# A third PSUM bank for the gated MLP's first-layer products, and the output weights' maximum ahead of the first group

## The chip, the cores and the metric

One core of one Trainium2 chip runs the whole kernel in one launch. The metric is the device time of that core in microseconds (us). Fewer is better. Three executions of the kernel before gave 2071.28, 2072.87 and 2073.14 us.

## The reference, cut to what matters

Three stages follow each other. The input of the first is 4 batches of 8 heads, 576 rows of 64 each. The second and third work on 2304 tokens of 512 features.

```python
# 1. attention with a threshold under each row's maximum
scores = q @ k.T / sqrt(64)
scores = where(scores >= max(scores) - tau, scores, -1e9)
x = softmax(scores) @ v                      # (2304, 512)
# 2. gated MLP
xn = x / rms(x) * rms_g
g, val = xn @ w_gate, xn @ w_val             # 512 -> 1536
x = (silu(g) * val) @ w_out                  # 1536 -> 512
# 3. eight experts, with weights P from a gate that is normalized eight times
out = sum(P[:, e] * (relu(x @ w1[e]) @ w2[e]) for e in range(8))
```

The change touches stage 2 and the place where it runs beside stage 1.

## The kernel before, in words

**Number format.** Every matrix is split into a high and a low fp16 part, and a product is three matmul passes (high by high, high by low, low by high; `passes`, line 546). The parts are scaled by powers of two. Each scale needs the largest value of a tensor over all partitions. `over_partitions` (line 127) gets it with one small matmul into PSUM and one VectorE maximum over it; from the second use on that matmul's tile has the tag `mx` in pool `psx`, with one buffer. This tile takes one bank of PSUM. All the kernel's small maxima share it: those of the keys and the values of each batch (`kmx`, `vmx`), of the output weights (`womx`), of the third stage's gate (`gmx`), and of its expert weights.

**Attention** runs tile by tile: 144 tiles, each of 128 query rows of one head (or of half as many rows of two heads). For a tile TensorE computes the scores `S` (line 303), VectorE their maximum (line 317), ScalarE the exponent `e` (line 321), VectorE the threshold and the sum (line 323), ScalarE the fp16 high part `hl` (line 328), POOL the low part (lines 329 and 330), a transposing DMA issued by SP turns it (`eT`, line 340), and four tiles later TensorE multiplies it by the values (`pv`, line 360). After 8 heads the row of 128 tokens is normalized and turned by another DMA into `xnT` (line 387).

**The gated MLP** works on groups of 256 tokens, nine in all. `mlp_in` (line 550) computes, for each of 12 blocks of 128 columns, `gv`: 12 matmuls for the gate and 12 for the value (line 557) into one PSUM bank of tag `mm` (pool `psm`, two buffers). ScalarE takes the tanh of the first half (line 565), and two VectorE operations form the gated product `u` (lines 566 and 567); the second of them is the last reader of the bank. ScalarE and POOL then split `u` into `tT` (lines 571 and 572). `mlp_out` (line 579) multiplies by the output weights into two tiles of the same tag `mm` (line 591). The first seven groups are given to the planner among the attention tiles; the last two come after attention and carry a `hook` that prepares expert weights.

**The weights' preparation** comes first. `prep_group` prepares the gate and value weights. `prep_out` (line 509) loads the output weights in 12 pieces (line 451, issued by SP), rebuilds them as 32-bit floats (lines 462 to 465), squares them on ScalarE for the row sums (line 517), forms the maximum `womx` (lines 519 to 527), and then scales and splits the 12 pieces (lines 534 to 536, VectorE, ScalarE and POOL).

**What sets the order.** The program is written down once, and a planner lays it out when the kernel is built: it takes for every engine the ready instruction with the lowest number, and numbers grow in the order of writing. It gives a PSUM buffer to a tile when one is free in its own estimate of the times. `high_priority(offset=n)` gives what stands in it numbers that are lower by `n`. Attention tiles get numbers as if no MLP work stood between them (`attention_order`), so that they go ahead of MLP work that is ready too. On the chip each engine then keeps this order and waits on semaphores. PSUM has eight banks: two tiles of two banks for `S`, one for `pv`, one for `mx`, two for `mm`.

Of the kernel before, what the change touches and what calls it, by code (L numbers as in the profile page):

```python
# [7 lines left out]
F32 = mybir.dt.float32  # L8
# [11 lines left out]
def kernel(  # L20
# [28 lines left out]
    E, _, FF = moe2_w1.shape  # L49
    P = 128  # L50
    KD = DM // P
    KF = DFF // P
# [8 lines left out]
    def small(shape, name, dt=F32, bufs=1):  # L61
        return p0.tile(shape, dt, tag=name, name=name, bufs=bufs)
# [63 lines left out]
    psx = ctx.enter_context(tc.tile_pool(name="psx", bufs=1, space=PSUM, side="left"))  # L126
# [12 lines left out]
    def all_max(col, name, first=False):  # L139

        return over_partitions(col.bitcast(BF16)[:, 1:2], ident, name, first)
# [26 lines left out]
    def norm_scale(sq, n, bits, name):  # L168

        return pow2_scale(sq, n, bits, name, 2.0**-60, True)  # L170
# [270 lines left out]
    NG = DFF // DM  # L441

    def words(src, name, tag="tT"):

        if tag == "tT":
            r = pw.tile([P, 4, 2, 2 * P], F16, tag=tag, name=name, bufs=4)
            r = r.rearrange("p f l n -> p (f l n)").bitcast(I32)
        else:
            r = pw.tile([P, 4, HD], F32, tag=tag, name=name)
            r = r.rearrange("p o d -> p (o d)").bitcast(I32)  # L450
        nc.sync.dma_start(out=r, in_=src)
        return r.rearrange("p (n w) -> p n w", w=2)

    def to_f32(dst, word, name):

        lw = pw.tile([P, 2, 2, HD], F16, tag="xs", name=name, bufs=2)  # L460
        lw = lw.rearrange("p o l n -> p (o l n)").bitcast(I32)
        A.activation(dst, word[:, :, 1].bitcast(F32), AF.Prelu, scale=2.0**-112, alpha=2.0**32)
        V.tensor_scalar(lw, word[:, :, 0], 29, None, ALU.logical_shift_right)
        di = dst.bitcast(I32)
        V.scalar_tensor_tensor(di, di, 3, lw, ALU.logical_shift_left, ALU.bitwise_or)
        return lw
# [42 lines left out]
    def prep_out():  # L509

        bits = moe_w_out.bitcast(I32)
        n = KF // NG
        om = small([P, KF], "om")
        for f in range(KF):
            wd = words(bits[f * P : (f + 1) * P, :], f"wo{f}", ("x2", "x2t")[f % 2])
            sq = to_f32(wo32[:, f], wd, f"wol{f}").bitcast(BF16)[:, 0:DM]
            A.activation(sq, wo32[:, f], AF.Square, accum_out=om[:, f : f + 1])
        for _ in range(2):
            V.tensor_tensor(
                om.rearrange("p (g f) -> p g f", g=NG),  # L520
                om.rearrange("p (g f) -> p g f", g=NG),
                igv.to_broadcast([P, NG, n]),
                ALU.mult,
            )
        om1 = small([P, 1], "om1")
        V.tensor_reduce(om1, om, AX.X, ALU.max)
        s, inv = norm_scale(all_max(om1, "womx"), 1, 9, "wout")
        V.tensor_scalar(ixs, inv, 2.0**10, None, ALU.mult)
        sf = small([P, NG], "wosf")
        V.tensor_scalar(sf, igv, s[:, 0:1], None, ALU.mult)  # L530
        rr = pw.tile([P, 4, HD], F32, tag="x2", name="wof")
        for f in range(KF):
            r = rr[:, f % 2 * 2 : f % 2 * 2 + 2].rearrange("p o d -> p (o d)")
            V.tensor_scalar(r, wo32[:, f], sf[:, f // n : f // n + 1], None, ALU.mult)
            A.activation(wo[:, f, 0, :], r, AF.Copy)
            G.tensor_tensor(wo[:, f, 1, :], r, wo[:, f, 0, :], ALU.subtract)

    NB = 2 * P
# [7 lines left out]
    def passes(n):  # L546

        return [(l, r, c) for c in range(n) for l, r in ((0, 0), (0, 1), (1, 0))]

    def mlp_in(j, hook=None):  # L550
        xt = xnT.pop(j)
        tT = []
        for f in range(KF):
            gv = psm.tile([P, 2, NB], F32, tag="mm", name=f"gv{j}_{f}")
            for a, w in enumerate((wg, wv)):
                for n, (l, r, kk) in enumerate(passes(KD)):
                    T.matmul(  # L557
                        gv[:, a, :],
                        lhsT=w[:, l, kk, f * P : (f + 1) * P],
                        rhs=xt[:, r * KD + kk, :],  # L560
                        start=n == 0,
                        stop=n == 3 * KD - 1,
                    )
            u = pw.tile([P, NB], F32, tag="u", name=f"u{j}_{f}", bufs=2)
            A.activation(u, gv[:, 0, :], AF.Tanh, scale=g32[f // (KF // NG)][:, 0:1])
            V.scalar_tensor_tensor(u, u, 1.0, gv[:, 0, :], ALU.add, ALU.mult)
            last = V.scalar_tensor_tensor(u, u, 2.0**-21, gv[:, 1, :], ALU.mult, ALU.mult)  # L567
            if f % 4 == 0:
                tq = pw.tile([P, 4, 2, NB], F16, tag="tT", name=f"tT{j}_{f}", bufs=4)
            t = tq[:, f % 4]  # L570
            A.activation(t[:, 0, :], u, AF.Copy)  # L571
            low = G.tensor_tensor(t[:, 1, :], u, t[:, 0, :], ALU.subtract)  # L572
            tT.append(t)
            if hook is not None:
                with tc.issue_after(last.ins), tc.issue_after(low.ins):
                    hook()
        return tT
# [65 lines left out]
    def attention_order():  # L643

        return tc.high_priority(offset=tc.cur_priority - first)
# [13 lines left out]
    def prepare(b, o):  # L659

        st = states[b]
        if o < NCH * H and o % H == 1:
            prep_q(st, o // H + 1)
        if b > 0 and o in (LAG - 3, LAG - 1):
            prep_v(st, (o - LAG + 3) // 2)
        if b + 1 == B:
            return
        nx = states[b + 1]
        early = b > 0
        if o == (4 if early else 20):  # L670
            nx["raw_k"] = load_raw("k", k, b + 1)
            nx["raw_v"] = load_raw("v", v, b + 1)
        for nm, o0, scales in (("k", 8 if early else 21, prep_k_scale), ("v", 11 if early else 24, prep_v_scale)):
            if o0 <= o < o0 + 3:
                row_norms(nx, nm, o - o0)
            if o == o0 + 2:
                scales(nx)
        o0 = 18 if early else 27
        if o0 <= o < o0 + 3:
            prep_k(nx, 0, o - o0)  # L680
        if o == 25:
            nx["raw_q"] = load_raw("q", q, b + 1)
        if o in (28, 29, 30):
            q_norms(nx, 2 * (o - 28), min(2 * (o - 27), NW))
        if o == 30:
            prep_q_scales(nx)
        if o == 32:
            prep_q(nx, 0)
        if o == 34:
            prep_k(nx, 1, 0)  # L690
        if o == 35:
            prep_k(nx, 1, 1)
            prep_k(nx, 1, 2)
# [20 lines left out]
    for t in range(len(row) + LAG):  # L714
        before = tc.cur_priority
        with attention_order():
            if t < len(row):
                b, c, heads, n, g = row[t]
                if n == 0:
                    g["sums"] = pa.tile([P, H], F32, tag="sums", name=f"sums{g['n']}", bufs=2)  # L720
                att_tile(states[b], c, heads, n, g)
                prepare(b, t % SLOTS)
            else:
                att_values(*waiting.pop(0))
                turn()
            done = list(ended)
            ended.clear()
            for g in done:
                (end_main if g["c"] < NCH else end_rem)(g)
        first += tc.cur_priority - before  # L730
        for g in done:
            i = g["i"]
            if i == 1:
                pse_cm.__exit__(None, None, None)
                psm = ctx.enter_context(
                    tc.tile_pool(name="psm", bufs=2, space=PSUM, side="right")
                )
                for gi in range(NG):
                    prep_group(gi)
                first = tc.cur_priority  # L740
                tT = mlp_in(0)
                prep_out()
                mlp_out(0, tT)
            elif i is not None and i % 2 == 1 and i < len(tiles) - 3:
                mlp_out(i // 2, mlp_in(i // 2))
# [211 lines left out]
    def hook():  # L957

        for call, *args in todo.pop(place[0], ()):
            call(*args)  # L960
        place[0] += 1

    j = NTL // 2 - 2
# [6 lines left out]
    tT = mlp_in(j + 1, hook)  # L970
# [206 lines left out]
    for hn in range(1, NE):  # L1177
        for which, base in ((1, 42 * (hn - 1) + 14 * (hn == 1)), (2, 42 * (hn - 1) + 21 + 13 * (hn == 1))):
            n = weight(which, hn, (lambda p: lambda: p)(w_pool(hn)))
# [5 lines left out]
    with tc.manual_schedule(engines={mybir.EngineType.PE}):  # L1185
        for k, (c, j) in enumerate(ahead):
            u, f = c // 2, c % 2
# [32 lines left out]
            while done < min(want, len(later)):  # L1220
                u, jj, j, _ = n = later[done]
# [51 lines left out]
```

## Time and profile before

| what | value |
|---|---|
| median of 3 executions | 2072.87 us (2071.28 to 2073.14) |
| the profiled execution's own time | 2072.64 us |
| its span, first to last instruction | 2070.8 us |
| TensorE (PE) busy | 1937.3 us, 94% |
| VectorE (DVE) busy | 1622.1 us, 78% |
| ScalarE (ACT) busy | 1297.6 us, 63% |
| POOL busy | 1351.4 us, 65% |

Attention fills the span from the start to about 597 us; the MLP's first matmul starts at 143.5 us and its last one at 728.2 us; the experts take the rest. A busy share is a mean over stages that have different limits, so the table says little by itself: what matters is, for the stretch in which the change acts, which engine stood idle and what released it. An operation is written as line, engine, operation, output <- inputs; what stands in square brackets behind an entry of the timeline is the idle time of the engine just before it and what ended it.

### The profile page before, as it was taken

Reading aid. Unit: us, or ns where it says so; the run is one execution under the profiler, and the core shown is the slowest. Engines: PE = TensorE matmul, PEld = TensorE weight load, DVE = VectorE, ACT = ScalarE, POOL = GpSimd, SP = SyncE. Lnnn points to the kernel's source line nnn. Section 1 sums busy time; section 2 is a strip of 40 time slices with the busy share of each in tenths; the row PEclk is TensorE's granted clock in tenths of the full one; section 3 lists DMA queues with packets and bytes.
Section 4 is the critical chain, followed back from the end, with each engine's and each line's share of the span. In section 5 each row is a group of like instructions: output and inputs, shape, how many; then the busy total and the mean of one; then the engine's idle time right before and its main releaser. Section 6 shows DMA issues by size and latency. Waiting matters only on the chain.

```text
span 2070.8 us, 43792 instructions
## 1 busy us (share of the span) xinstructions
PE 1937.3 (94%) x16462; PEld 1445.0 (70%) x16462; DVE 1622.1 (78%) x3364; ACT 1297.6 (63%) x2804; POOL 1351.4 (65%) x1412
## 2 busy tenths in 40 slices
PE   1558899899999998999999999999999999999998
PEld 0246676777777766777777777777777777777777
DVE  6998777778754546998888888888887888888865
ACT  6998778878753365657555555555555555555542
POOL 0457664666654476777677777776777777777754
PEclk9569999999999999999999999999999999999999
DMA  9987878977748665334434433444443434334332
GB/s 296 261 177 128 163 160 147 184 129 139 129 83 213 144 158 169 110 118 143 128 120 134 131 116 119 130 131 127 128 139 122 122 117 143 120 120 128 105 97 82
DMA packets 373093, 290.46 MB, mean 140 GB/s; under 512 B 286160, under 2 KB 299344, under 8 KB 372880
## 3 DMA queue, kind: packets, MB, share of 16 engines
q1 hardware_dynamic: 371712, 285.81, 53.6%
q8 instruction: 129, 2.11, 0.4%
q0 software_dynamic: 640, 1.84, 0.3%
q14 instruction: 84, 0.69, 0.1%
q10 hardware_dynamic: 528, 0.02, 0.0%
HBM read 195.71 MB, written 21.23 MB: 105 GB/s over the span
## 4 chain that ended last, share of the span: by engine, by line
PE 65%; DVE 3%; POOL 1%; DMA 1%; issue 1%; ACT 1%; SPq 0%; DVEq 0%; POOLq 0%; ACTq 0%
PE P L1127 30%; PE X L1059 17%; PE Z L1059 13%; PE gv L557 3%; PE x L591 2%; DVE w L766 1%; DMA xo<-x2d 1%; DVE acc L1141 0%; SPq L871 0%; DVE h L1038 0%; PE logits L913 0%; DVE lg L1005 0%; POOL w2s L833 0%; DVE w1m L790 0%; POOL h L1038 0%
## 5 line engine op out<-in xcount | busy, mean ns | idle before, releaser
L1127 PE MATMUL P<-w,h 128*128 128x256 f16 x6048 | 769.9, 273 | 2.7 <-DVE acc L1141 1.8
L1127 PEld LDWEIGHTS <-h 128*128 128x128 f16 x6048 | 591.4, 98 | 145.7 <-issue 9.8
L1059 PEld LDWEIGHTS <-w 128*128 128x128 f16 x4032 | 394.6, 98 | 195.6 <-issue 4.6
L1137 DVE SCALAR_TENSOR_TENSOR acc<-P,coef,acc 128x256 f32<-128x256 f32 x882 | 409.7, 477 | 81.7 <-PE P L1127 73.0
L1059 PE MATMUL X<-xo,w 128*128 128x384 f16 x2304 | 437.7, 327 | 1.3 <-ACT u2b L1079 0.9
L1059 PE MATMUL Z<-xo,w 128*128 128x384 f16 x1728 | 327.7, 326 | 1.5 <-DMA xo<-x2d 1.5
L329 POOL TENSOR_TENSOR hl<-e,hl 128x512 f16<-128x512 f32 x144 | 172.9, 1201 | 193.7 <-ACT hl L328 135.6
L557 PE MATMUL gv<-xnT,wg 128*128 128x256 f16 x1296 | 162.9, 274 | 14.7 <-DVE u L567 13.4
L557 PE MATMUL gv<-xnT,wv 128*128 128x256 f16 x1296 | 165.0, 273 | 0.0
L557 PEld LDWEIGHTS <-wg 128*128 128x128 f16 x1296 | 124.7, 98 | 33.7 <-issue 16.0
L591 PE MATMUL x<-wo,tT 128*128 128x512 f16 x648 | 144.2, 379 | 0.0
L323 DVE SCALAR_TENSOR_TENSOR e<-S,nt,e 128x576 f32<-128x576 f32 x144 | 116.5, 811 | 28.5 <-ACT e L321 28.0
L557 PEld LDWEIGHTS <-wv 128*128 128x128 f16 x1296 | 125.5, 98 | 14.7
L317 DVE TENSOR_REDUCE nt<-S 128x1 f32<-128x576 f32 x144 | 106.7, 750 | 25.1 <-PE S L303 22.8
L360 PE MATMUL pv<-vs,eT 128*128 128x64 f16 (+1 forms) x2240 | 97.1, 200 | 30.9 <-DMA eT<-hl 30.8
L360 PEld LDWEIGHTS <-eT 128*128 128x128 f16 (+1 forms) x2240 | 87.3, 105 | 52.9 <-DMA eT<-hl 40.3
L572 POOL TENSOR_TENSOR tT<-u,tT 128x256 f16<-128x256 f32 x108 | 74.9, 695 | 69.7 <-ACT tT L571 69.6
L321 ACT ACTIVATE e<-S,nt,c 128x576 f32<-128x576 f32 x144 | 117.4, 818 | 0.0
L591 PEld LDWEIGHTS <-tT 128*128 128x128 f16 x648 | 62.1, 98 | 70.7
L328 ACT ACTIVATE hl<-e 128x576 f16<-128x576 f32 x144 | 96.8, 677 | 21.3 <-DMA eT<-hl 10.4
L303 PE MATMUL S<-kT,qT 128*128 128x288 f16 (+1 forms) x320 | 65.2, 310 | 26.3 <-DVE e L323 19.7
L766 DVE SCALAR_TENSOR_TENSOR w<-w1r,w_s,w 128x512 f16<-128x512 f32 x64 | 84.1, 1328 | 7.1 <-ACT w L765 7.0
(2536 smaller groups left out, 3623.2 us busy)
## 6 DMA issues: line engine op xcount, KB each, us to landing
xo<-x2s SPq DMA_DIRECT2D x319, 384.0 KB, 3.1
w1r<-in_moe_w_dram SPq DMA_DIRECT2D x17, 1024.0 KB, 5.0
w2r<-in_moe_w_dram SPq DMA_DIRECT2D x17, 1024.0 KB, 6.1
x2s<-xo SPq DMA_DIRECT2D x17, 384.0 KB, 2.8
wgatew<-in_moe_w_gate_dram SPq DMA_DIRECT2D x12, 512.0 KB, 5.6
wo<-in_moe_w_out_dram SPq DMA_DIRECT2D x12, 512.0 KB, 4.6
wvalw<-in_moe_w_val_dram SPq DMA_DIRECT2D x12, 512.0 KB, 5.1
qX<-qT SPq DMA_DIRECT2D x40, 128.0 KB, 2.7
```

What stands on the lines that cost most here:

```text
L317: V.tensor_reduce(mx, sv, AX.XY, ALU.max)
L321: A.activation(ev, sv, AF.Exp, bias=nt[:, 0:1], scale=st["c2"][:, c : c + 1])
L323: V.scalar_tensor_tensor(ev, sv, nt[:, 1:2], ev, ALU.is_ge, ALU.mult, accum_out=sums[:, slot : slot + 1])
L328: A.activation(hl[:, 0:S], e, AF.Copy)
L329: G.tensor_tensor(hl[:, S + REM :], e[:, 0 : NCH * P], hl[:, 0 : NCH * P], ALU.subtract)
L360: T.matmul(o, lhsT=a, rhs=r, start=n == 0, stop=n == len(mm) - 1)
L557: T.matmul(gv[:, a, :], lhsT=w[:, l, kk, f * P : (f + 1) * P], rhs=xt[:, r * KD + kk, :], start=n == 0, stop=n == 3 * KD - 1,)
L591: T.matmul(ps, lhsT=tT[f][:, l, o : o + P], rhs=wo[:, f, r, :], start=n == 0, stop=n == 3 * KF - 1,)
L766: V.scalar_tensor_tensor(dst[1], src, s, dst[0], ALU.mult, ALU.subtract)
L1059: T.matmul(ps, lhsT=w[:, a, l, kk, f * P : (f + 1) * P], rhs=xb[:, r * 2 + kk, :], start=n == 0 and j in (0, 1, 3), stop=n == 5, skip_grou ...
L1127: T.matmul(ps, lhsT=hs[u, ao, f][:, l, jj * P : (jj + 1) * P], rhs=w2[h][:, bo, r, f, :], start=n == 0 and j in (0, 1, 3), stop=n == 5, sk ...
L1137: main[True] = V.scalar_tensor_tensor(y, ps, coef[h][:, i : i + 1], y, ALU.mult, ALU.add)
```

## The change

`mlp_in` without a hook, that is in the first seven groups, takes every third block's `gv` tile (f = 2, 5, 8 and 11) from pool `psx` with the tag `mx` instead of from `psm`. `prep_out` is cut in two: the first part ends with the maximum and returns the scale, the second (`split_out`) scales and splits. The first part is written ahead of the first group's `mlp_in`, whose instructions get the same numbers that the first part starts with; the second part stays behind it.

```diff
@@ prep_out
         s, inv = norm_scale(all_max(om1, "womx"), 1, 9, "wout")
         V.tensor_scalar(ixs, inv, 2.0**10, None, ALU.mult)
+        return s
+
+    def split_out(s):
+
+        n = KF // NG
         sf = small([P, NG], "wosf")
         V.tensor_scalar(sf, igv, s[:, 0:1], None, ALU.mult)
         rr = pw.tile([P, 4, HD], F32, tag="x2", name="wof")
@@ mlp_in
         for f in range(KF):
-            gv = psm.tile([P, 2, NB], F32, tag="mm", name=f"gv{j}_{f}")
+            if hook is None and f % 3 == 2:
+                gv = psx.tile([P, 2, NB], F32, tag="mx", name=f"gv{j}_{f}", bufs=1)
+            else:
+                gv = psm.tile([P, 2, NB], F32, tag="mm", name=f"gv{j}_{f}")
@@ the main loop
                 first = tc.cur_priority
-                tT = mlp_in(0)
-                prep_out()
+                p0_ = tc.cur_priority
+                so = prep_out()
+                with tc.high_priority(offset=tc.cur_priority - p0_):
+                    tT = mlp_in(0)
+                split_out(so)
                 mlp_out(0, tT)
```

## Rows read from the trace of the kernel before

**Rows 1.** Windows by stage: stretch, its length, busy us, clock, DMA share.

```profile
143.00:182.00 39.00, 32.46 (x377) 28.33 (x375) 34.12 (x87) 37.59 (x92) 33.58 (x38) 1.00 0.57 108
240.00:620.00 380.00, 362.62 (x4028) 278.59 (x4027) 283.94 (x660) 290.01 (x676) 234.40 (x324) 1.00 0.76 139
620.00:740.00 120.00, 119.15 (x909) 84.30 (x908) 59.25 (x132) 47.23 (x99) 55.63 (x69) 1.00 0.67 162
860.00:2071.00 1211.00, 1203.31 (x9259) 904.35 (x9256) 999.02 (x1945) 681.91 (x1418) 864.40 (x806) 1.00 0.40 122
```

**Rows 2.** Waits of TensorE, 140 to 620 us: total, times, longest.

```profile
PE gv L557 <- DVE u L567: 12.7, 13, 2.6
PE pv L360 <- DMA eT<-hl: 12.1, 15, 1.6
PE S L303 <- DVE e L323: 2.4, 4, 1.3
```

**Rows 3.** The tile gv: last reader of the bank.

```profile
L567 DVE SCALAR_TENSOR_TENSOR u<-u,gv x108: 404/420/422, 151.8 to 714.1; 128x256 f32<-128x256 f32 x108
```

**Rows 4.** Waits of TensorE, 140 to 240 us, then 240 to 620 us.

```profile
PE gv L557 <- DVE u L567: 6.1, 6, 2.6
...
PE gv L557 <- DVE u L567: 6.6, 7, 1.5
```

**Rows 5.** Timeline of TensorE, first group: start, length, instruction.

```profile
143.54 1.48 PE L557 MATMUL gv<-xnT,wg 128*128 128x256 f16 x12
...
146.16 0.27 PE L557 MATMUL gv<-xnT,wg 128*128 128x256 f16 x1
...
157.64 1.47 PE L557 MATMUL gv<-xnT,wg 128*128 128x256 f16 x12 [2.58 <-DVE u L567]
```

**Rows 6.** Timelines of SP and TensorE where the second group starts.

```profile
216.17 1.33 SPq L387 DMA_TRANSPOSE xnT<-xn  x1
...
219.40 1.49 PE L557 MATMUL gv<-xnT,wg 128*128 128x256 f16 x12 [1.08 <-DMA xnT<-xn]
```

**Rows 7.** Timeline of TensorE, two later waits and what follows each.

```profile
240.81 1.47 PE L557 MATMUL gv<-xnT,wg 128*128 128x256 f16 x12 [0.80 <-DVE u L567]
...
245.57 0.58 PE L360 MATMUL pv<-vs,eT 128*128 128x64 f16 x14 [1.36 <-DMA eT<-hl]
...
383.05 1.47 PE L557 MATMUL gv<-xnT,wg 128*128 128x256 f16 x12 [1.22 <-DVE u L567]
...
392.23 0.58 PE L360 MATMUL pv<-vs,eT 128*128 128x64 f16 x14 [1.60 <-DMA eT<-hl]
```

**Rows 8.** Timeline of TensorE where its clock falls once.

```profile
525.47 2.63 PE L557 MATMUL gv<-xnT,wg 128*128 128x256 f16 x12 [1.40 <-DVE u L567]
...
529.75 0.41 PE L303 MATMUL S<-kT,qT 128*128 128x288 f16 x2
```

**Rows 9.** Windows around it, columns as in rows 1.

```profile
522.00:526.00 4.00, 1.60 (x23) 1.08 (x21) 3.96 (x6) 1.33 (x4) 1.42 (x3) 0.95 0.40 83
526.00:530.00 4.00, 4.00 (x25) 3.00 (x24) 3.59 (x9) 2.52 (x7) 2.33 (x4) 0.62 1.05 177
```

**Rows 10.** Output weights: loads, rebuilding, squares, the maximum's matmul, the first piece's split.

```profile
L451 SPq DMA_DIRECT2D wo<-in_moe_w_out_dram x12: 328/460/575, 15.1 to 129.2; - x12
...
L465 DVE SCALAR_TENSOR_TENSOR wo<-wo,wol x12: 676/686/1636, 93.5 to 134.8; 128x512 int32<-128x512 int32 x12
L517 ACT ACTIVATE wol<-wo x12: 612/626/637, 95.0 to 136.5; 128x512 bf16<-128x512 f32 x12
...
L134 PE MATMUL womxp<-ident,om x1: 230/230/230, 138.3 to 138.3; 128*128 128x128 bf16 x1
...
L534 DVE TENSOR_SCALAR wof<-wo,wosf x12: 430/526/1367, 140.8 to 169.0; 128x512 f32<-128x512 f32 x12
```

**Rows 11.** Small maxima from 150 to 640 us: their matmuls, the keys' VectorE maximum.

```profile
L134 PE MATMUL vmxp<-ident,vmm x3: 219/219/220, 154.8 to 401.5; 128*128 128x128 bf16 x3
...
L134 PE MATMUL kmxp<-ident,kmm x2: 219/224/230, 215.9 to 355.7; 128*128 128x128 bf16 x2
L134 PE MATMUL gmxp<-ident,gm x1: 219/219/219, 436.5 to 436.5; 128*128 128x128 bf16 x1
...
L136 DVE TENSOR_REDUCE kmx<-kmxp x2: 285/289/293, 220.8 to 356.0; 128x1 f32<-128x128 f32 x2
```

## The prediction, made before the changed kernel was run

> **What bounds the kernel now.** I read the windows by stage first. From 860 us to the end TensorE is busy 1203.31 of 1211 us, and from 620 to 740 us, where the last MLP groups run alone, 119.15 of 120 us [rows 1]. There only less TensorE work, or work done earlier, can shorten the span. The stretch in which the change acts is the one before: from 240 to 620 us TensorE is busy 362.62 of 380 us, from 143 to 182 us 32.46 of 39 us [rows 1]. In that stretch MLP matmuls fill what attention leaves, and what is not done by 597 us is done after it, back to back. So a microsecond of TensorE idle time that goes before 620 us comes off the end, provided attention and the MLP's inputs keep up.
>
> Next the waits of TensorE between 140 and 620 us. Three kinds make up nearly all: a gv tile waits for the bank that VectorE's second product reads last, 12.7 us in 13 waits; values wait for a turned tile (eT), 12.1 us in 15; scores wait for the release of S, 2.4 us in 4 [rows 2]. Only the first kind is what a third bank addresses. It is 0.6% of the span, and the whole direct prize.
>
> **The third bank.** One gv block takes TensorE 146.16 - 143.54 = 2.62 us [rows 5]. With two banks, block f+2 may start once block f's second product has ended; that product lasts 0.42 us [rows 3], so a wait means that VectorE or ScalarE reached the block late in their queues. With three banks the release has one block more, at least 2.62 us. The longest wait is 2.58 us [rows 5], so in the old order of instructions every one of the 13 would vanish. What that brings at the end I count by place [rows 4].
>
> First place, 143 to 182 us: 6.1 us in 6 waits. ScalarE is busy 37.59 of 39 us there, TensorE 32.46 [rows 1]: ScalarE still serves the output weights' split beside attention and tanh. A further bank does not raise a rate that ScalarE sets; it lets TensorE get ahead by at most one block, 2.62 us. And that lead has to survive until the second group starts: its first matmul waits 1.08 us for an input that SP issues at 216.17 us [rows 6], so a first group that ends sooner meets the same late input unless attention comes sooner too. The bounds are 0 and -6.1 us; I take -1.0, near zero, because of the row at 219.40.
>
> The Trainium skill, "Perfetto Trace Analysis", section "Identifying the Most-Contended Engine", takes ScalarE's occupancy as a fair measure of its limit and says to work on the fullest engine first. By that the first place would be worth nothing, and the sum below would be 1.0 us smaller; by the waits alone it would be 5.1 us larger.
>
> Second place, 240 to 620 us: 6.6 us in 7 waits. Here no other engine is full (ScalarE 290.01, VectorE 283.94 of 380 us) [rows 1]. A wait is worth its length only if nothing late follows. After two of the seven, at 240.81 (0.80 us) and 383.05 (1.22 us), a value matmul waits for eT within 10 us, for 1.36 and 1.60 us [rows 7]. Its scores were made four attention tiles earlier, ahead of the gv wait, so eT will not come sooner, and these waits grow by what was gained. The other five are worth 6.6 - 0.80 - 1.22 = 4.58 us. The bounds are 0 (all five meet a late eT further on) and -6.6; I take -4.6.
>
> **The clock.** At 525.47 us a gv block after a wait of 1.40 us takes until 529.75, 4.28 us in place of 2.62 [rows 8, 5]. The granted clock of 526 to 530 us is 0.62, a mix of the levels 1.2 and 2.4 GHz; in the 4 us before TensorE was busy 1.60 us only [rows 9]. Without the 1.40 us of waiting TensorE is fuller ahead of that point and the clock may stay up. Bounds 0 and -1.7 us; I take half, -0.8.
>
> **New sharing.** From now on 28 gv tiles (four of each of seven groups) use the bank of the small maxima. In their time six maxima follow after 150 us: three of the values, two of the keys, one of the gate [rows 11]. None of their matmuls waits for a bank now. One can hold its bank long: a key maximum's matmul at 215.9 us is read only at 220.8, since VectorE had other work first [rows 11]. The price of one collision is bounded by 0 (the planner puts the small matmul where the bank is free, on the chip too) and by the longest wait for a gv bank, 2.58 us [rows 5]. I take one collision in all at the mean wait, 12.7 / 13 = 0.98 us [rows 2], so +1.0. Behind a waiting small matmul stand all TensorE work and, on VectorE, what follows the maximum: attention's next reductions. The scales themselves are not urgent: the batch that needs them begins many tiles later.
>
> **The moved maximum.** What moves ahead in number are 12 loads on SP, 24 ScalarE and 24 VectorE operations on them with their 12 sum readings, the few VectorE operations of the maximum and its matmul. On the chip they stand ahead of the first gv already: the last load is issued at 129.2 us, the last square starts at 136.5, the maximum's matmul at 138.3, the first split at 140.8 [rows 10], and gv starts at 143.54 [rows 5]. No DMA or POOL work of the first group is passed, since `mlp_in` issues none of the former and its POOL work stands behind the gv; POOL's work of the split stays behind in number. Against attention tiles from the twenty-first on the moved part gains rank, which can matter for its last load or two (0.46 us of SP each) [rows 10]. I cost the move at nothing; its cover is the late input of the first group. If that cover were gone, the third gv block could start only after the maximum.
>
> **The sum.** -1.0 - 4.6 - 0.8 + 1.0 = -5.4 us. Against the profiled execution's own 2072.64 us (span 2070.8, and 1.84 us around it; 0.23 us under the median) this gives **2067.2 us**, 0.26% less. Since the planner lays out the whole stretch anew, the 14.5 us of eT and score waits [rows 2] are dealt again; I leave their sum as it is.
>
> **Rivals.**
>
> *Attention keeps the pace (no change).* If ScalarE in the first place and eT later set the pace, each gv wait that goes comes back as an eT or input wait. For it: such a next wait stands in place already [rows 6, 7]. Against: ScalarE and VectorE have a quarter of their time free from 240 us on [rows 1], and after 525.47 nothing late follows for long. All bank terms are 0; 2072.6 us.
>
> *The shared bank (slower).* The small matmul of a maximum is queued on TensorE behind a gv block in the same bank, whose release hangs on VectorE. At the longest gv wait six maxima cost 6 x 2.58 = 15.5 us; with the other terms (-6.4) the time is 2072.64 + 9.1 = 2081.7 us. It beats the gain from 6.4 / 6 = 1.07 us each. For it: the 4.9 us that a maximum held its bank. Against: only six occasions.
>
> The Trainium skill, "PSUM — Partial Sum Buffer", section "Engine vs sequencer instructions", says that VectorE's queue is strictly first in, first out. By that the maximum's reading, once late, would hold attention's reductions too; no row of this trace shows it.
>
> *Everything comes through (more).* All 12.7 us and 1.7 us of clock go, nothing collides: -14.4, 2058.2 us. This needs attention to come sooner by as much, which ScalarE's 37.59 of 39 us speaks against.
>
> The part that doesn't do what it says is the moved maximum: it is ahead already.
>
> **How the numbers follow.** A measurement of this kernel tells about 0.2% from no change, here 4.1 us. My forecast has a chance of 0.42, no change 0.28, the shared bank 0.18, everything 0.12. Of the forecast's 0.42 I put 0.04 inside 4.1 us. So faster 0.38 + 0.12 = 0.50, the same 0.28 + 0.04 = 0.32, slower 0.18. The likeliest case alone spans 2062 to 2070. The range goes from 2058 (all terms at their best) to 2080, most of the way to the shared bank's 2081.7.
>
> **What would show it.** In the changed kernel's waits of TensorE from 140 to 620 us the gv wait for VectorE should be under 4 us, the eT wait 12 to 16 us, a wait of a small maximum or of gv for one at most 1 or 2 us. The second group's first matmul should still wait for its input, at 217 to 220 us. Attention's last value matmul should come a few us before 597. Stretches after 620 us should keep their lengths. I am wrong if the eT waits double, if small maxima appear in TensorE's waits with over 6 us, or if attention itself ends more than 10 us away from 597.

## The result, and the profile after

The changed kernel takes 2102.02 us (median of 4 runs, 2100.99 to 2103.28), the kernel before 2073.01 us beside it: a ratio of 1.0139, 95% interval 1.0122 to 1.0157. It is 29 us **slower**, where 0.26% faster was forecast and 2080 us was the upper end of the range.

First the page of the changed kernel: its span, and the row of the engines' busy times.

```profile
span 2099.2 us, 43781 instructions
...
PE 1949.3 (93%) x16462; PEld 1449.2 (69%) x16462; DVE 1613.5 (77%) x3364; ACT 1299.5 (62%) x2804; POOL 1352.3 (64%) x1412
```

The span grew by 2099.2 - 2070.8 = 28.4 us. TensorE's busy time grew by 12.0 us with the same number of matmuls, so part of them ran slower; the other 16.4 us are time in which it stood idle. The windows of the changed kernel, columns as in rows 1, say where.

```profile
143.00:182.00 39.00, 37.16 (x419) 32.38 (x417) 32.58 (x73) 37.20 (x91) 35.21 (x42) 0.96 0.57 98
240.00:620.00 380.00, 345.30 (x3757) 259.09 (x3755) 277.50 (x653) 293.08 (x679) 231.57 (x318) 0.96 0.79 145
620.00:740.00 120.00, 119.34 (x1025) 92.09 (x1024) 60.19 (x141) 47.27 (x100) 54.01 (x70) 1.00 0.65 157
```

In the first place TensorE does more than before (37.16 of 39 us, before 32.46) [rows 1]. From 240 to 620 us it does less: 345.30 us busy instead of 362.62, at a granted clock of 0.96 instead of 1.00. From 620 us on it is as full as before, with the work that was left over. The worst 40 us are these, in the changed kernel:

```profile
280.00:320.00 40.00, 23.26 (x260) 14.99 (x259) 28.14 (x67) 32.11 (x72) 27.05 (x38) 0.74 0.95 191
```

and in the kernel before:

```profile
280.00:320.00 40.00, 38.31 (x433) 30.64 (x431) 29.75 (x74) 32.75 (x82) 26.21 (x37) 1.00 0.73 135
```

TensorE stands idle for 16.7 of 40 us, 15.0 more than before, and falls to the lower of its levels (1.2 of 2.4 GHz) for a part of them. That is nearly as much as the 16.4 us of new idle time in the whole kernel. Now the waits of TensorE in the changed kernel from 140 to 640 us (total, times, longest).

```profile
PE pv L360 <- DMA eT<-hl: 21.3, 21, 3.3
PE S L303 <- DVE e L323: 10.3, 12, 1.8
PE gv L565 <- DVE u L575: 2.9, 2, 1.8
...
PE kmxp L134 <- DVE u L575: 1.5, 1, 1.5
PE vmxp L134 <- DVE xm L608: 1.2, 1, 1.2
```

The gv wait fell from 12.7 to 2.9 us, as the edit intended; the waits for eT and for S grew from 14.5 to 31.6 us [rows 2]. The small maxima themselves wait 2.7 us in all. So by the waits for the bank alone the sharing looks harmless. The damage is in a view that shows *when* they run. Their matmuls in the changed kernel:

```profile
L134 PE MATMUL kmxp<-ident,kmm x3: 217/220/220, 206.1 to 444.1; 128*128 128x128 bf16 x3
...
L134 PE MATMUL vmxp<-ident,vmm x3: 220/220/230, 207.4 to 518.7; 128*128 128x128 bf16 x3
...
L134 PE MATMUL gmxp<-ident,gm x1: 220/220/220, 660.8 to 660.8; 128*128 128x128 bf16 x1
```

and what they read, the key maximum of each partition, from the view of its tile:

```profile
L191 DVE TENSOR_REDUCE kmm<-km x3: 149/156/156, 144.2 to 374.7; 128x1 f32<-128x3 f32 x3
```

The input for batch 1's key maximum is there at 144.2 us, and its matmul runs at 206.1. In the kernel before it ran here:

```profile
146.27 0.22 PE L134 MATMUL kmxp<-ident,kmm 128*128 128x128 bf16 x1
```

Batch 3's key maximum runs at 444.1 instead of 355.7, its value maximum at 518.7 instead of 401.5, the gate's at 660.8 instead of 436.5 [rows 11]. Of the 62 us by which batch 1's key matmul runs behind its input, TensorE stood waiting for it for 1.5 us only: the planner had put it that late in its queue. The timeline of TensorE in the changed kernel shows the entry right before it:

```profile
203.12 1.47 PE L565 MATMUL gv<-xnT,wv 128*128 128x256 f16 x12
```

These are the last 12 matmuls of block 11, the last block of the first group and the last of its four in the shared bank. Counted over the whole trace, batch 1's key and value maxima stand behind 12 gv blocks, batch 2's behind 24, batch 3's key maximum behind 48 and its value maximum behind 60: each time behind whole groups. In the kernel before these were 1, 3, 12, 22, 36 and 45 blocks. I read it so: all blocks of a group can be asked for as soon as the group's input is there, and whatever asks for the bank later comes after them, though attention's numbers are lower. The planner's own steps are not on record; the positions in these kernels are what speaks for it.

What that does to attention is seen in the timeline of the changed kernel.

```profile
190.85 0.42 PE L303 MATMUL S<-kT,qX 128*64 128x288 f16 x4
...
206.06 0.22 PE L134 MATMUL kmxp<-ident,kmm 128*128 128x128 bf16 x1 [1.47 <-DVE u L575]
...
222.17 0.65 PE L303 MATMUL S<-kT,qT 128*128 128x288 f16 x4
```

Batch 0's last scores are at 190.85 us, batch 1's first ones at 222.17: a hole of 31 us without scores. In its second half the keys are scaled, split and turned, 16.1 us from the maximum on. In the kernel before batch 0 ends and batch 1 starts so, with a hole of 7 us:

```profile
192.99 0.41 PE L303 MATMUL S<-kT,qX 128*64 128x288 f16 x4
...
199.75 0.41 PE L303 MATMUL S<-kT,qT 128*128 128x288 f16 x2
```

Batch 1 starts 22.4 us later. The MLP fills the hole at first, with its first two groups, but the input of a further group is what attention makes. In the changed kernel the second group's last matmuls and the third group's first ones are these:

```profile
281.99 1.89 PE L599 MATMUL x<-wo,tT 128*128 128x512 f16 x8
...
323.32 1.61 PE L565 MATMUL gv<-xnT,wg 128*128 128x256 f16 x12 [0.22 <-DMA xnT<-xn]
```

In the kernel before the third group starts at 290.77 us. For the 39 us between the two rows TensorE has attention's work alone, and falls idle and slow.

### The profile page after: what moved, and what is told of

Its sections match the earlier page's. It is cut to its first block, busy times and chain, and to the rows that moved or that the text cites. A ratio compares the mean times of both kernels' runs of the same rounds, so it can differ in the third digit from the quotient of the medians.

```text
span 2099.2 us, 43781 instructions
## 1 busy us (share of the span) xinstructions
PE 1949.3 (93%) x16462; PEld 1449.2 (69%) x16462; DVE 1613.5 (77%) x3364; ACT 1299.5 (62%) x2804; POOL 1352.3 (64%) x1412
## 4 chain that ended last, share of the span: by engine, by line
PE 67%; DVE 3%; POOL 1%; DMA 1%; issue 1%; ACT 1%; SPq 0%; DVEq 0%; POOLq 0%
PE P L1138 29%; PE X L1070 16%; PE Z L1070 12%; PE gv L565 4%; PE x L599 3%; DVE w L777 1%; PE pv L360 1%; DMA xo<-x2d 1%; PE S L303 0%; DVE acc L1152 0%; DMA eT<-hl 0%; SPq L882 0%; DVE h L1049 0%; POOL tT L580 0%; PE logits L924 0%
## 5 line engine op out<-in xcount | busy, mean ns | idle before, releaser
L360 PE MATMUL pv<-vs,eT 128*128 128x64 f16 (+1 forms) x2240 | 101.3, 203 | 41.0 <-DMA eT<-hl 39.3
L317 DVE TENSOR_REDUCE nt<-S 128x1 f32<-128x576 f32 x144 | 106.8, 751 | 32.3 <-PE S L303 31.6
L328 ACT ACTIVATE hl<-e 128x576 f16<-128x576 f32 x144 | 96.8, 677 | 22.4 <-DMA eT<-hl 15.0
L574 DVE SCALAR_TENSOR_TENSOR u<-u,gv 128x256 f32<-128x256 f32 x108 | 44.9, 417 | 62.6 <-ACT u L573 61.3
```

The costliest lines, as they stand in the source:

```text
L317: V.tensor_reduce(mx, sv, AX.XY, ALU.max)
L328: A.activation(hl[:, 0:S], e, AF.Copy)
L360: T.matmul(o, lhsT=a, rhs=r, start=n == 0, stop=n == len(mm) - 1)
```

## The experiments

All ratios are to runs of the kernel before beside them. "Blocks" are gv blocks ahead in TensorE's queue.

**e1: the maxima out of the bank.** Everything of the change stays, but the key and value maxima of batches 1 to 3 take a buffer of the score tiles.

```diff
-        if first:
+        if first == "S":
+            ps = psa.tile([P, 2, 512], F32, tag="S", name=name + "p", bufs=2)[:, 0, 0:P]
+        elif first:
...
-        return all_max(m, nm + "mx", st["b"] == 0)
+        return all_max(m, nm + "mx", st["b"] == 0 or "S")
```

> The changed kernel, but the key and value maxima of batches 1 to 3 take a buffer of the score tiles instead of the bank that the third gv tile now uses. Theory (the keys' and values' maxima come late, because the bank is given in the order of asking and all four gv blocks of a group ask first): the small matmuls of batch 1 stand at about 150 to 160 us again instead of 206, attention ends near 597 us, the time is 2062 to 2074 us. Rival (a third gv bank by itself lets MLP work crowd attention out of ScalarE, VectorE and TensorE): stays at 2090 us or more.

Measured: 2073.2 us, ratio 0.9995 (0.9985 to 1.0004). Batch 1's maxima run at 148.4 and 162.7 us, its scores start at 200.19. All of the 29 us is gone, though the third bank is there: what costs is the sharing with these maxima. As to the time the rival is out. The expectation missed attention's end: its last value matmuls start at 612.46 us (before 600.85), and the whole time does not show it.

**e2: the third bank without the move.**

```diff
-                p0_ = tc.cur_priority
-                so = prep_out()
-                with tc.high_priority(offset=tc.cur_priority - p0_):
-                    tT = mlp_in(0)
-                split_out(so)
+                tT = mlp_in(0)
+                split_out(prep_out())
```

> The changed kernel without its second part: the output weights' maximum is written behind the first group again. Theory: that maximum now joins the same queue for the bank behind group 0's four blocks, near 200 us instead of 138, so the split of the output weights and the first group's second layer come later still: 2105 to 2130 us. Rival (the moved preparation is what costs): 2070 to 2076 us.

Measured: 2092.62 us, ratio 1.0095 (1.008 to 1.011). The small matmuls of this run:

```profile
L134 PE MATMUL kmxp<-ident,kmm x3: 216/220/220, 192.3 to 439.1; 128*128 128x128 bf16 x3
...
L134 PE MATMUL womxp<-ident,om x1: 216/216/216, 191.7 to 191.7; 128*128 128x128 bf16 x1
```

The output weights' maximum joined the queue behind 12 blocks as expected (191.7 us in place of 138.3), but the time was better than with the move, not worse. With the output weights' split still to come, ScalarE and VectorE got through the first group sooner (VectorE is busy 27.36 of the 39 us from 143 to 182 us, in the change 32.58), so the key maximum came at 192.3 instead of 206.1 and batch 1 started at 208.67. The expectation had the queue right and its price wrong. Batch 1 starts only 8.9 us later than in the kernel before, and the loss is two thirds of the change's: the start alone does not measure it. The hole without scores, 22.8 us here (185.90 to 208.67) against 31 in the change and 7 before, goes with it better.

**e3: the move alone**, no third bank.

> The kernel before with only the second part of the change (output weights' maximum ahead of the first group, no third bank). Theory: no difference, 2070 to 2076 us, since that work ran ahead of the first group already. Rival (the moved preparation is what costs): 2090 us or more.

Measured: 2079.27 us, ratio 1.0024 (1.0015 to 1.0034). The output weights' maximum runs at 137.9 us, as before, and batch 1 starts at 200.70. There is a small loss all the same, 5 us, between the two expectations. Its cause is not shown; the gv wait is 14.0 us in 10 waits, and the order of instructions is a new one from there on. It cannot explain the 29 us.

**e4: the third bank in groups 5 and 6 only** (`j >= 5` added to its condition), when the last key and value maximum is gone.

> The changed kernel with the third bank in groups 5 and 6 only, after the last key and value maximum has gone. Theory: no loss is left and a microsecond or two of gv waits goes: 2068 to 2074 us. Rival (the third bank itself crowds attention out, in each group alike): about two sevenths of the loss of 29 us, 2078 to 2084 us.

Measured: 2076.48 us, ratio 1.001 (1.0001 to 1.002): between the two expectations again, and less than what the move alone costs. It shows no share of the 29 us.

**e5: lateness alone.** The kernel before, two gv banks, nothing moved; key and value maxima ask for one of the two gv banks.

```diff
-            ps = psx.tile([P, P], F32, tag="mx", name=name + "p", bufs=1)
+            ps = (psm.tile([P, 2, NB], F32, tag="mm", name=name + "p")[:, 0, 0:P]
+                  if name in ("kmx", "vmx") else psx.tile([P, P], F32, tag="mx", name=name + "p", bufs=1))
```

> The kernel before, still with two banks for gv and nothing moved, but the key and value maxima of batches 1 to 3 ask for one of the two gv banks and so stand behind all gv blocks of a group that have asked already. Theory (lateness of the maxima is enough by itself): batch 1's maxima near 200 us, a hole in the scores around 190 to 220 us as in the changed kernel, 2090 to 2110 us. Rival (it takes the third bank, too): 2070 to 2080 us.

Measured: 2103.53 us, ratio 1.0139 (1.0123 to 1.0155), the same as the change. Its small matmuls and its scores around 200 us:

```profile
L134 PE MATMUL kmxp<-ident,kmm x3: 219/219/220, 208.9 to 460.9; 128*128 128x128 bf16 x3
```

```profile
189.83 0.41 PE L303 MATMUL S<-kT,qX 128*64 128x288 f16 x4
224.90 0.65 PE L303 MATMUL S<-kT,qT 128*128 128x288 f16 x4
```

The maxima stand behind 12, 24, 48 and 60 blocks again, in another bank. Late maxima are enough by themselves, without a third bank and without the move.

**e9: the third bank in the first group only** (`j == 0`).

> The changed kernel with the third bank in the first group only. Then batch 1's key and value maxima are late by some 55 us, those of batches 2 and 3 are not. Theory (the hole before batch 1 is the main cost): 2085 to 2100 us, a hole of some 25 to 30 us without scores near 200 us. Rival (batch 3's late values are the main cost): 2076 to 2082 us.

Measured: 2097.63 us, ratio 1.0114 (1.0095 to 1.0132). Batch 1's maxima run at 208.6 and 209.9 us, batch 1 starts at 224.68. Four blocks of one group make 1.14 of the change's 1.39%.

**e8: the third bank from group 4 on** (`j >= 4`).

> The changed kernel with the third bank from group 4 on. Batch 3's value maximum then waits for group 4's last block (some 510 us in place of 401), all other key and value maxima are in time. Theory (a late maximum costs only where attention has nothing else to do): values late beyond the lag of four tiles, 2077 to 2088 us. Rival (only keys matter, since scores go on without values): 2072 to 2078 us, as with groups 5 and 6.

Measured: 2077.23 us, ratio 1.0011 (1.0001 to 1.0022). Batch 3's value maximum runs at 491.5 us, behind 60 blocks, and the time is that of e4, where no key or value maximum is late. It lies in both expected ranges, but the cost that my theory wanted is not there. The 90 us are counted from the kernel before; batch 3's scores start at 468.82 us, so its value maximum comes 23 us after them. That much costs nothing that can be seen.

**e13 and e14: keys or values.** The change, with only the key maxima (e13) or only the value maxima (e14) in a buffer of the score tiles.

> The changed kernel with only the key maxima of batches 1 to 3 in a buffer of the score tiles; the value maxima still queue behind the gv blocks. Theory (the late keys make the hole, since scores cannot start without them, and late values do little): no hole near 200 us, 2072 to 2082 us. Rival (values late by 50 us stop the softmax's multiplication and with it everything): 2090 us or more.

Measured: 2064.81 us, ratio 0.9955 (0.9941 to 0.997). Its small matmuls, and its waits of TensorE from 140 to 640 us:

```profile
L136 PE MATMUL kmxp<-ident,kmm x3: 219/219/220, 150.8 to 373.6; 128*128 128x128 bf16 x3
...
L136 PE MATMUL vmxp<-ident,vmm x3: 219/220/220, 199.2 to 484.5; 128*128 128x128 bf16 x3
```

```profile
PE pv L362 <- DMA eT<-hl: 11.2, 12, 1.9
PE S L305 <- DVE e L325: 8.0, 9, 2.2
PE gv L567 <- DVE u L577: 2.8, 3, 1.7
```

> The changed kernel with only the value maxima in a buffer of the score tiles; the key maxima still queue. Theory: the hole of some 30 us stays, 2092 to 2106 us. Rival (values are what stops it): 2072 to 2082 us.

Measured: 2098.25 us, ratio 1.0118 (1.0105 to 1.0131):

```profile
L136 PE MATMUL vmxp<-ident,vmm x3: 230/230/290, 159.1 to 413.8; 128*128 128x128 bf16 x3
...
L136 PE MATMUL kmxp<-ident,kmm x3: 216/220/220, 205.3 to 440.6; 128*128 128x128 bf16 x3
```

This settles it. With the values' maxima queued and the keys' in time the loss turns into a gain of 0.45%, below the expected range; with the keys' queued and the values' in time (batch 1 starts at 218.39) most of the loss stays. The late keys are the cause. That late values are harmless in general is not shown: in e13 batch 1's value maximum runs at 199.2 us and its first value matmul at 221.47, so it was still in time. And e13 beats both kernels; the gv wait is 2.8 us, as in the change. Whether the third bank makes this gain is asked next.

**e10, e11, e15: is there more in it?** e10 has the third bank in all seven groups, nothing moved, and the maxima of keys, values and output weights in a buffer of the score tiles.

> Third bank in all seven groups, nothing moved, and the maxima of keys, values and output weights in a buffer of the score tiles. Theory (the move alone cost 5 us, the third bank with maxima in time gains about 5): 2064 to 2071 us. Rival (each such edit only deals the order anew, by 5 us either way, and the first group's lead is lost at the second group's late input): 2071 to 2079 us, gv waits for VectorE under 4 us all the same.

Measured: 2078.17 us, ratio 1.0021 (1.001 to 1.0032): the rival. The gv wait is 1.1 us, and the waits for S are 11.3 us, 2.4 in the kernel before.

e11 is e10 from group 1 on.

> Third bank in groups 1 to 6, nothing moved, the maxima of keys, values and output weights in a buffer of the score tiles. Theory (the first group's lead is lost at the second group's late input, the later groups' is not): 2066 to 2073 us, faster than with the third bank in all groups. Rival (scatter of a new order, 5 us either way): 2074 to 2081 us.

Measured: 2076.85 us, ratio 1.0014 (1.0004 to 1.0024), the rival again.

e15 is the kernel before with a third bank in groups 5 and 6, nothing moved.

> The kernel before with a third bank in groups 5 and 6 only and nothing moved. Up to those groups the order is the one of before, so no new deal of the order can hide the gain. Theory: the gv waits after 500 us (1.4 us) and the fall of the clock there go, 2071 to 2074.5 us, the same as before or up to 0.15% faster. Rival (the new deal outweighs it here too): over 2077 us.

Measured: 2073.2 us, ratio 1.0 (0.9991 to 1.0008): no difference. From 480 us on no gv wait is left, as expected, but waits for S of 4.7 us stand there instead, and the clock still falls: it is 0.84 from 526 to 530 us.

## Why the prediction was wrong

**The step that failed** is the term "new sharing", and in it the bound: the price of a collision was to lie between 0, "the planner puts the small matmul where the bank is free", and 2.58 us, the longest wait for a gv bank. That bound comes from waits of TensorE, that is from the chip running late against its queue. The planner did put the small matmul where the bank is free; I never asked *how late* that is when four blocks of a group ask for the bank first. It was 62 us for batch 1's keys (144.2 to 206.1). The +1.0 us of the sum measured some +29: all of it is gone in e1, all of it is there in e5 without a third bank. The count was short, too. The rows of the small maxima began at 150 us, so "six" left out batch 1's key maximum at 146.27 us, though gv tiles start at 143.54. It is a seventh, and the one that e9 and e14 together show to cost the most.

**The second half of that step** was the sentence that the scales are not urgent since the batch begins many tiles later. Two rows of the trace of before bound it: batch 1's key maximum stands at 146.3 us there and its first scores at 199.75, so there were 53 us at most. The changed kernel shows that 16.1 of them are the work from the maximum to the scores, which leaves a slack of 37 us. The maximum came 60 us later; 22.4 us of that were over the slack, and by so much batch 1 started later. I had counted tiles where a subtraction of two rows was needed.

**The slower rival** named the right place, the bank of the small maxima, with a chance of 0.18, and the wrong mechanism: six waits of up to 2.58 us on TensorE, 2081.7 us. Six such waits are not there; 2.7 us in 2 are.

**The signs.** Of the three signs of being wrong one came: attention's last value matmuls start at 629.40 us, in the kernel before at 600.85 (the 597 that I had given is some 4 us early). The eT waits grew to 21.3 us without doubling, and the small maxima waited 2.7 us, not over 6. The second group's first matmul runs at 207.99 us without a wait, not at 217 to 220: the first group's lead was there, and the hole took what came after it.

**The third bank's own terms.** The gv wait fell to 2.9 us as forecast (under 4). What it brings could be seen only with the keys in time, and then it differed: 0.9995 in e1, 0.9955 in e13, 1.0021 in e10, all with gv waits of at most 3.2 us. The forecast of -6.4 us before the sharing lies between them, so no run shows it. The doubt about the first place was right for e1. The second layer of the first group starts there at 184.72 us instead of 196.1, and then meets a late tT; the second group starts at 221.11, before at 219.40. From e1's timeline, and its window from 182 to 240 us:

```profile
216.97 2.74 PE L601 MATMUL x<-wo,tT 128*128 128x512 f16 x6 [4.83 <-ACT tT L581]
```

```profile
182.00:240.00 58.00, 48.78 (x521) 32.68 (x519) 42.84 (x96) 43.91 (x97) 29.94 (x41) 0.91 0.86 165
```

In e13 the same stretch is fuller, at the upper level of the clock:

```profile
182.00:240.00 58.00, 53.61 (x594) 38.44 (x591) 46.71 (x113) 47.16 (x104) 33.81 (x46) 1.00 0.90 168
```

Weighted with the clock that is, as an estimate, 53.61 - 48.78 x 0.91 = 9.2 us more work in e13, not far from the 10.7 us between the two spans. Why the order of e13 fits better there is not settled; no run was made for it.

**The clock term** was small and went the other way. The fall at 526 us was to go with a gv wait; instead the clock fell for longer behind the hole, at 280 us. In e15 the gv wait went and the clock fell all the same.

**The moved maximum** was costed at nothing. Alone it cost 5 us (e3), for a cause that is not shown. With the shared bank it did something: without it the output weights' maximum waits until 191.7 us (e2). That I missed, for the same reason as the keys; even so e2 is the faster of the two.

**A new order has a price of its own.** Eight runs have the keys in time and differ in small edits: 1.0024, 1.0021, 1.0014, 1.0011, 1.001, 1.0, 0.9995 and, with e13, 0.9955. I left the sum of the other waits as it was; "dealt again" should have been a term of its own, by these runs between 5 us more and 9 us less. That it is the new order that makes them differ is argued, not shown.

**Left open:** the 5 us between e9 or e14 and the whole change, at the edge of the intervals; and whether e13's gain is the third bank's or its order's.

## What to carry to other kernels

Before a long-lived tile is put into the bank of a short one, look up for each short user when its input is ready, when its result is needed, and who can have asked for the bank in between: the waiting line costs the sum of their lifetimes, not one of them. The Trainium skill, "Perfetto Trace Analysis", section "Matmuls", advises to rotate independent matmul groups through different PSUM banks. Here that took the gv wait from 12.7 to 2.9 us, and so far the trace agrees, but the kernel still lost 29 us until the keys' maximum was given another place. And when a wait view looks clean but the kernel is slower, compare the times at which the same instruction runs in both kernels: a matmul that the planner queued 60 us later shows next to no wait, here 1.5 us.

## What the runs showed that I had not expected

TensorE's clock fell in the hole's wake: from 280 to 320 us it was busy 23.26 of 40 us, at a granted clock of 0.74, a mix of 1.2 and 2.4 GHz. From these two numbers an estimate of what the clock cost there is 23.26 x (1 - 0.74) = 6.0 us. That is half of the 12.0 us by which its busy time grew over the whole kernel at the same 16462 matmuls; the rest lies elsewhere and was not followed. So the late keys cost not only idle time but slower work beside it.
